# Which engines issue the output stores of the last seven chunks, and which engine evicts the last chunk, in a Fourier-mixing and snake-MLP kernel

## The chip, the cores and the metric

The kernel runs on one core of a Trainium2 chip. The metric is the device time of one execution in microseconds (us). "Faster" and "slower" compare the kernel after the change with the kernel before it. The engines are called here as the profile calls them: PE (TensorE) multiplies matrices, DVE (VectorE) and ACT (ScalarE) work on rows of elements, POOL (GpSimd) does elementwise work and issues DMAs, and SP (SyncE) only issues DMAs and waits. DMAs can be issued by SP, ACT and POOL.

## The reference

The inputs are `x` of 8 x 3008 x 256 and a complex filter for each frequency and channel. Each channel is filtered along the sequence, and the 24,064 tokens that come out go through a two-layer MLP with a snake activation.

```python
X = np.fft.rfft(x, axis=1)
F = (filt_r + 1j * filt_i)[None, :, :]
y = np.fft.irfft(X * F, n=x.shape[1], axis=1)      # 8 x 3008 x 256

h = y.reshape(24064, 256) @ w_in                   # 256 x 2048
s = np.sin(alpha * h)
g = h + s * s / (alpha + 1e-09)
out = (g @ w_out).astype(np.float32)               # 2048 x 256
```

## The kernel before

The transforms are done as matrix products with tables, in two stages of 47 and 64 points, one batch after the other (class `Spectral`). Between the stages the data goes through DRAM scratch buffers, so the spectral part has its own DMAs on SP and POOL. Its result is `y`: channels on partitions, tokens along columns, with room for one pair of batches.

The MLP takes the tokens in 48 chunks, 12 for each pair of batches, each of 512 columns (one of 384 in each pair). For a chunk `k`, `hidden(k, jb)` runs for 16 blocks of 128 hidden units. PE multiplies `w1` by the chunk's columns into the PSUM tile `ph` (L601), ACT takes the cosine as a shifted sine into `cos_all` (L605), and DVE forms `v` from both (L606). The square of the sine is rewritten with the cosine of the doubled angle, and the factors are folded into `w1` and `w2`. `project(k, u)` then multiplies `v` by `w2` into the PSUM tile `po` (L620), 16 matmuls for each tile of 128 tokens. Two token tiles share a `po` tile, which is evicted by one copy into an SBUF tile `o` (L628). Two `po` buffers and three `o` buffers rotate.

The order on every engine is that of the program, written out by hand. A main loop steps through `hidden` of chunk `k` and `project` of chunk `k - 1`, half a block at a time, and between these it puts the steps of the spectral part at due times from a list (`pending`, `slot`). After the last `hidden` there are eight steps with `project` of the last chunk alone. In these, token tiles 2 and 3 are taken in reverse order, and each has a `po` tile, a copy and stores of its own (`final`).

`store` (from L645; its DMAs are issued on L663) writes one tile of 128 tokens to the output. Tokens stand in `y` in the order of the transform, not of the output. A tile is therefore cut into parts whose rows lie at a fixed stride in DRAM, and each part is one DMA with 1 KB per row. There are 2 to 4 parts in a tile, and which engine issues them is the argument `queues`. From the second pair of batches on, a part of `r` row pairs has 2r rows; all stores that the change touches are of this kind. Before, all stores are issued by POOL, except those of the last chunk: its tiles 0 and 1 use SP and POOL by turns, and its tiles 2 and 3 use SP, ACT and POOL by turns, larger parts first.

The program ends on L785: each engine runs a DRAIN, signals, and waits at a barrier that POOL gathers. SP's signal comes after it has waited, one semaphore after another, for the stores that are still out.

Of the kernel before, what the change touches and what calls it, by code (L numbers as in the profile page):

```python
# [71 lines left out]
def kernel(  # L72
# [10 lines left out]
    nc = tc.nc  # L83
# [55 lines left out]
    for h in range(2):  # L139
        nc.sync.dma_start(out=x32[:, 4 * C * h:4 * C * h + 4 * C],  # L140
                          in_=bass.AP(tensor=x.tensor, offset=x.offset + 4 * h * C, ap=[[32 * C, 96], [1, 4 * C]]))
# [182 lines left out]
    al, rest, rec = [w2_cols[0:16, 256 * i:256 * i + 256].bitcast(FP32) for i in range(3)]  # L324
# [32 lines left out]
    for g in range(2):  # L357
        gs = slice(12 * g, 12 * g + 12)
        for k, filt in enumerate((filt_r, filt_i)):
            for q in range(2):  # L360
                if (g, k, q) == (0, 1, 1):
# [3 lines left out]
                    out=f_t[k][64 * k + 32 * q:64 * k + 32 * q + 32, gs, :],  # L365
                    in_=bass.AP(tensor=filt.tensor, offset=filt.offset + off,
                                ap=[[N1 * C, 32], [step, 12], [1, C]]))
# [20 lines left out]
    def one_between():  # L388

        if between:  # L390
            between.pop(0)()
# [143 lines left out]
    for jb in range(0, 16, 8):  # L535
        ins = nc.sync.dma_start(out=w_out32[:, jb:jb + 8],
                                in_=moe_w_out[128 * jb:128 * jb + 1024].rearrange("(b p) c -> p b c", p=128))
# [41 lines left out]
    for step in ([(weights_in, g) for g in range(3)] + [(s1.load_x, 0), (weights_in, 3), (s1.load_x, 1),  # L579
# [8 lines left out]
    chunks = [(pb, c0, 384 if c0 == 2560 else 512) for pb in range(B // 2)  # L588
              for c0 in [*range(0, 2561, 512), *range(2944, 2 * S, 512)]]

    v = {}
    pso = {}
# [17 lines left out]
    def project(k, u):  # L610

        pb, c0, n = chunks[k]
        t, half = divmod(u, 2)
        final = k == len(chunks) - 1 and t > 1
        if final:
            t = 5 - t
        if (t % 2 == 0 or final) and half == 0:
            pso[k] = ops.tile([128, 2, C], FP32, name=f"po_{k}_{t}", tag="o")
        for jb in range(8 * half, 8 * half + 8):
            nc.tensor.matmul(out=pso[k][:, t % 2, :], lhsT=v[k][:, jb, 128 * t:128 * t + 128],  # L620
                             rhs=w2[:, jb, :], start=(jb == 0), stop=(jb == 15))
            if jb % 2:
                one_between()
        last = 128 * (t + 1) == n
        if half == 1 and (t % 2 == 1 or last or final):
            i0 = t % 2 if final else 0
            o = opool.tile([128, 2, C], FP32, name=f"o_{k}_{t}", tag="o")
            nc.scalar.copy(out=o[:, i0:t % 2 + 1, :], in_=pso[k][:, i0:t % 2 + 1, :])  # L628
            for i in range(i0, t % 2 + 1):
                store(o[:, i, :], pb, c0 + 128 * (t - t % 2 + i),  # L630
                      (nc.sync, nc.scalar, nc.gpsimd) if final else (nc.sync, nc.gpsimd) if k == len(chunks) - 1 else
                      (nc.gpsimd,))

    def load_half_table():

# [4 lines left out]
    def runs(cnt):  # L640

        whole = cnt if max(d for d in range(1, 17) if cnt % d == 0) > 7 else cnt - cnt % 16
        return [(0, whole), (whole, cnt - whole)] if 0 < whole < cnt else [(0, cnt)]

    def store(o_blk, pb, col, queues):  # L645

        p, parts = 0, []
        while p < 128:
            odd, rest = divmod(col + p, S)
            n2, row = divmod(rest, NR)  # L650
            cnt = min(128 - p, NR - row)
            t0 = (2 * pb + odd) * S + 32 * row
            if 2 * pb + odd < TILED:
                parts += [(i, rows, t0 + n2 + 32 * r0, p + r0, [[32 * C, rows]])
                          for i, (r0, rows) in enumerate(runs(cnt))]
            else:
                parts += [(i, 2 * rows, t0 + 31 - n2 + 64 * r0, p + 2 * r0, [[64 * C, rows], [(2 * n2 + 1) * C, 2]])
                          for i, (r0, rows) in enumerate(runs(cnt // 2))]
            p += cnt
        if len(queues) == 3:  # L660
            parts = [(i, *part[1:]) for i, part in enumerate(sorted(parts, key=lambda part: -part[1]))]
        for i, rows, t0, p0, ap in parts:
            queues[i % len(queues)].dma_start(  # L663
                out=bass.AP(tensor=out.tensor, offset=out.offset + t0 * C, ap=[*ap, [1, C]]),
                in_=o_blk[p0:p0 + rows, :])
# [81 lines left out]
    for k in range(len(chunks) + 1):  # L747
        for j in range(8):
            if k < len(chunks) and step > 0:
                hidden(k, 2 * j)  # L750
                hidden(k, 2 * j + 1)
            slot(step)
            if k > 0:
                n_half = 2 * (chunks[k - 1][2] // 128)
                for u in range(n_half * j // 8, n_half * (j + 1) // 8):
                    project(k - 1, u)
            slot(step + 0.5)
            step += 1
# [31 lines left out]
```

## Time and profile before

| What | Value |
|---|---|
| runs before | 782.67 us median of 3 (781.52, 782.67, 783.74) |
| profiled execution, first to last instruction (span) | 779.9 us |
| the median of the runs above that span | 2.8 us |
| PE busy | 762.2 us (98% of the span) |
| DVE / ACT / POOL busy | 656.8 / 612.0 / 416.1 us |
| output stores issued by POOL (L663) | 608, mean 561 ns |
| evictions of `po` by ACT (L628) | 97, mean 590 ns |

A span runs from the first to the last instruction on the core. No time of its own is listed for the profiled execution beside this span, so sums are made against 779.9 us and then carried over to the median of the runs, which lies 2.8 us above it. In the tables of the profile, "busy" leaves out instructions of the sequencers: a `q` after an engine's name (SPq, ACTq, POOLq) marks these, among them DMA issues of SP and ACT, waits on semaphores and DRAIN.

### The profile page before, as it was taken

What the parts mean: (1) busy time and instruction counts of PE and PEld (TensorE: products, weight loads), DVE (VectorE), ACT (ScalarE), POOL (GpSimd) and SP (SyncE); (2) the same over time, 40 slices, a digit from 0 to 9 for tenths busy, and PEclk for the clock granted to TensorE, in tenths of its full rate; (3) what the DMA queues carried; (4) which work ended last, traced back from release to release, by engine and by line L of the source; (5) the groups of instructions that cost most, each with busy time, mean ns of one, the idle gap of its engine ahead of it and who ended that gap; (6) DMA issues with size and microseconds to landing.
All of it is one profiled execution on the core that took longest, in us unless ns stands there. A gap on an engine that the chain in (4) does not pass through costs nothing.

```text
span 779.9 us, 17214 instructions
## 1 busy us (share of the span) xinstructions
PE 762.2 (98%) x6039; PEld 517.1 (66%) x6039; DVE 656.8 (84%) x1170; ACT 612.0 (78%) x1206; POOL 416.1 (53%) x727
## 2 busy tenths in 40 slices
PE   8999999999999999999999999999999999999994
PEld 4757766666666667666666666666666666766663
DVE  7887998899988889988889888898888888777771
ACT  6798887898787878878788878888788777777771
POOL 6455455644636456554656555653555545544553
PEclk9999999999999999999999999999999999999998
DMA  9945678854865448553575437654364232411111
GB/s 227 283 103 164 141 164 247 216 131 112 218 147 125 111 94 206 136 135 93 128 191 125 127 98 180 179 133 108 82 156 106 68 86 70 120 36 35 41 41 42
DMA packets 80201, 101.49 MB, mean 130 GB/s; under 512 B 19552, under 2 KB 58494, under 8 KB 80114
## 3 DMA queue, kind: packets, MB, share of 16 engines
q0 software_dynamic: 30096, 50.41, 27.3%
q1 hardware_dynamic: 49719, 49.86, 24.1%
q8 instruction: 47, 0.77, 0.4%
q14 instruction: 40, 0.33, 0.1%
q10 hardware_dynamic: 299, 0.13, 0.1%
HBM read 56.15 MB, written 46.66 MB: 132 GB/s over the span
## 4 chain that ended last, share of the span: by engine, by line
PE 89%; DVE 4%; DMA 2%; ACT 1%; POOL 1%; issue 1%; POOLq 0%; SPq 0%
PE po L620 39%; PE ph L601 39%; DVE v L606 3%; PE pd L316 2%; PE pb L243 2%; PE pa L222 2%; PE pc L293 1%; DMA x<-in_x_dram 1%; DMA d<-t_h 1%; POOL out_dram L663 1%; PE pc L513 1%; ACT cos_all L605 1%; PE warm L437 1%; PE pb L491 1%; DMA cos_all<-in_x_dram 0%
## 5 line engine op out<-in xcount | busy, mean ns | idle before, releaser
L606 DVE SCALAR_TENSOR_TENSOR v<-cos_all,ph 128x512 f16<-128x512 f32 (+1 forms) x768 | 482.8, 672 | 95.9 <-ACT cos_all L605 92.2
L605 ACT ACTIVATE cos_all<-ph 128x512 f32<-128x512 f32 (+1 forms) x768 | 413.7, 599 | 100.2 <-PE ph L601 99.8
L663 POOL DMA_DIRECT2D out_dram<-o x608 | 337.2, 561 | 287.1 <-ACT o L628 256.1
L601 PE MATMUL ph<-y,w 128*128 128x512 f16 (+1 forms) x1536 | 389.0, 375 | 1.3 <-DVE v L606 1.1
L620 PE MATMUL po<-w,v 128*128 128x256 f16 x3008 | 389.3, 273 | 0.0
L620 PEld LDWEIGHTS <-v 128*128 128x128 f16 x3008 | 290.1, 98 | 84.2 <-issue 1.1
L601 PEld LDWEIGHTS <-w 128*128 128x128 f16 x1536 | 143.2, 98 | 113.9 <-issue 19.0
L628 ACT COPY o<-po 128x512 f32<-128x512 f32 (+1 forms) x97 | 57.3, 590 | 13.1 <-PE po L620 9.5
L246 ACT CAST xf<-pb 128x512 f16<-128x512 f32 x84 | 50.9, 606 | 1.3 <-PE pb L243 1.0
L185 ACT CAST y<-pd 128x376 f16<-128x376 f32 (+1 forms) x86 | 41.9, 489 | 12.2 <-PE pd L316 8.8
L160 POOL DMA_DIRECT2D x<-in_x_dram x48 | 25.7, 540 | 38.0 <-DVE v L606 26.6
L185 ACT CAST t_h<-pa 128x512 f16<-128x512 f32 (+1 forms) x60 | 32.9, 589 | 12.7 <-PE pa L222 11.5
L316 PEld LDWEIGHTS <-t_a 96*128 96x128 f16 x448 | 31.4, 97 | 12.7
L264 DVE TENSOR_TENSOR p<-p,xs 128x512 f16<-128x512 f16 x84 | 35.7, 425 | 2.9
L263 DVE TENSOR_TENSOR xs<-xs,filt_t 128x512 f16<-128x512 f16 x84 | 35.2, 419 | 2.1 <-DMA xs<-xf 1.8
L257 DVE TENSOR_TENSOR p<-xf,filt_t 128x512 f16<-128x512 f16 x84 | 35.1, 418 | 0.0
L185 ACT CAST gt<-pc 128x512 f16<-128x512 f32 x54 | 28.1, 594 | 8.4 <-PE pc L293 8.4
L187 DVE CAST t_h<-pa 128x512 f16<-128x512 f32 (+1 forms) x52 | 33.5, 683 | 0.2
L243 PE MATMUL pb<-t,d_t 128*128 128x256 f16 x168 | 32.1, 273 | 0.0
L316 PE MATMUL pd<-wh_t,t_a 96*128 96x94 f16 x384 | 31.8, 204 | 0.0
L235 POOL DMA_DIRECT2D t<-d x28 | 24.5, 877 | 11.9 <-DMA d<-t_h 10.9
L243 PEld LDWEIGHTS <-d_t 128*128 128x128 f16 x168 | 16.3, 98 | 14.3
(69 smaller groups left out, 274.7 us busy)
## 6 DMA issues: line engine op xcount, KB each, us to landing
t<-d POOLq DMA_DIRECT2D x28, 384.0 KB, 5.2
xs<-xf SPq DMA_DIRECT2D x168, 64.0 KB, 2.7
t_a<-d SPq DMA_DIRECT2D x28, 384.0 KB, 5.3
x<-in_x_dram POOLq DMA_DIRECT2D x50, 188.0 KB, 4.7
d<-t_h SPq DMA_DIRECT2D x48, 192.0 KB, 5.1
d<-gt SPq DMA_DIRECT2D x36, 256.0 KB, 3.6
out_dram<-o POOLq DMA_DIRECT2D x106, 64.0 KB, 2.1
out_dram<-o POOLq DMA_DIRECT2D x32, 80.0 KB, 3.5
```

Source lines behind the costliest of these rows:

```text
L185: marks["act"] = nc.scalar.copy(out=dst, in_=src)
L243: nc.tensor.matmul(out=ps[:, i, :], lhsT=d_t[:, s, :], rhs=self.t2[s // 6][:, s % 6, :], start=True, stop=True)
L246: nc.scalar.copy(out=self.xf[u], in_=ps)
L263: nc.vector.tensor_tensor(out=xs, in0=xs, in1=f_t[1][:, 2 * u:2 * u + 2, :], op=ALU.mult)
L264: nc.vector.tensor_tensor(out=p, in0=p, in1=xs, op=ALU.add)
L316: nc.tensor.matmul(out=psv[:, i, :], rhs=wi_t if self.b < TILED else wh_t, start=True, stop=True, lhsT=t4_h[ch // 2][0:NK, n0 % 16 + i, cb ...
L601: nc.tensor.matmul(out=ps[:, 0:n], lhsT=w1[:, cb, jb * 128:jb * 128 + 128], rhs=y_cols[:, cb, c0:c0 + n], start=(cb == 0), stop=(cb == 1))
L605: nc.scalar.activation(out=cs[:, 0:n], in_=ps[:, 0:n], func=AFT.Sin, bias=float(np.pi / 2))
L606: marks["snake"] = nc.vector.scalar_tensor_tensor(out=v[k][:, jb, 0:n], in0=cs[:, 0:n], scalar=-1.0, in1=ps[:, 0:n], op0=ALU.add, op1=ALU. ...
L620: nc.tensor.matmul(out=pso[k][:, t % 2, :], lhsT=v[k][:, jb, 128 * t:128 * t + 128], rhs=w2[:, jb, :], start=(jb == 0), stop=(jb == 15))
L628: nc.scalar.copy(out=o[:, i0:t % 2 + 1, :], in_=pso[k][:, i0:t % 2 + 1, :])
L663: queues[i % len(queues)].dma_start(out=bass.AP(tensor=out.tensor, offset=out.offset + t0 * C, ap=[*ap, [1, C]]), in_=o_blk[p0:p0 + rows, :])
```

## The change

The stores of chunks 41 to 47 (the last seven, `rest < 7`) are no longer issued by POOL. SP issues them alone, except for the last six token tiles: those of tiles 2 and 3 of chunk 46 and of all four tiles of chunk 47 are dealt to SP and ACT by turns, larger parts first. The three copies that evict the last chunk move from ACT to DVE. In the built program 78 stores leave POOL; SP issues 70 more than before (78 instead of 8) and ACT 8 more (10 instead of 2). The last instruction of POOL's own work is then the last store of chunk 40. On SP the new stores stand behind all transfers of the spectral part, and on ACT behind its last cosine. The three copies stand on DVE behind its last `v`. The order on PE is unchanged.

```diff
@@ project
-            nc.scalar.copy(out=o[:, i0:t % 2 + 1, :], in_=pso[k][:, i0:t % 2 + 1, :])
+            rest = len(chunks) - 1 - k
+            copy = nc.vector.tensor_copy if rest == 0 else nc.scalar.copy
+            copy(out=o[:, i0:t % 2 + 1, :], in_=pso[k][:, i0:t % 2 + 1, :])
             for i in range(i0, t % 2 + 1):
                 store(o[:, i, :], pb, c0 + 128 * (t - t % 2 + i),
-                      (nc.sync, nc.scalar, nc.gpsimd) if final else (nc.sync, nc.gpsimd) if k == len(chunks) - 1 else
-                      (nc.gpsimd,))
+                      (nc.sync, nc.scalar) if rest == 0 or (rest == 1 and t > 1) else
+                      (nc.sync,) if rest < 7 else (nc.gpsimd,))
@@ store
-        if len(queues) == 3:
+        if len(queues) > 1:
             parts = [(i, *part[1:]) for i, part in enumerate(sorted(parts, key=lambda part: -part[1]))]
         for i, rows, t0, p0, ap in parts:
             queues[i % len(queues)].dma_start(
```

## The prediction

> **What bounds the kernel now.** I read the page first: which engine is full, and whether it stays full to the end.
>
> ```profile
> PE 762.2 (98%) x6039; PEld 517.1 (66%) x6039; DVE 656.8 (84%) x1170; ACT 612.0 (78%) x1206; POOL 416.1 (53%) x727
> PEclk9999999999999999999999999999999999999998
> ```
>
> PE is the bound and its clock is full. The busy times by stretch split the part that the change touches (columns: length, then busy us and instruction count of PE, PEld, DVE, ACT and POOL, the clock, the DMA share, GB/s):
>
> ```profile
> 689.00:762.00 73.00, 73.00 (x533) 49.84 (x532) 54.09 (x86) 52.02 (x100) 37.52 (x66) 1.00 0.14 39
> 762.00:780.00 18.00, 7.67 (x71) 6.63 (x68) 1.29 (x2) 2.42 (x6) 6.77 (x12) 0.80 0.16 44
> ```
>
> From 689 to 762 us PE is busy for all of 73.00 us. POOL's 66 stores there take 37.52 us beside it, and DVE and ACT have about 20 us of slack each. So nothing that POOL, DVE or ACT save in that stretch shortens it. The last stretch is different: PE works 7.67 of 18 us. What ends when, there, is in the timeline:
>
> ```profile
> 762.30 7.37 PE L620 MATMUL po<-w,v 128*128 128x256 f16 x66
> 763.60 6.19 POOL L663 DMA_DIRECT2D out_dram<-o  x11 [4.03 <-ACT o L628]
> 766.21 0.59 ACT L628 COPY o<-po 128x512 f32<-128x512 f32 x1 [2.91 <-PE po L620]
> 766.82 5.64 SPq L663 DMA_DIRECT2D out_dram<-o  x8
> ...
> 769.70 0.37 ACT L628 COPY o<-po 128x256 f32<-128x256 f32 x1 [1.38 <-DMA out_dram<-o]
> 770.11 1.40 ACTq L663 DMA_DIRECT2D out_dram<-o  x1
> 770.37 0.57 POOL L663 DMA_DIRECT2D out_dram<-o  x1 [0.58 <-ACT o L628]
> ```
>
> PE ends at 769.67, the last copy at 770.07, and the last store is issued by SP until 772.46. The span ends at 779.9. Nothing in this view fills the rest, so I asked for the instructions of the program's end (L785) from 762 to 779 us:
>
> ```profile
> L785 SPq EVENT_SEMAPHORE  x9: 28/28/28, 772.5 to 774.4; - x9
> L785 SPq DRAIN  x2: 7/7/7, 774.4 to 774.5; - x2
> L785 DVEq DRAIN  x1: 836/836/836, 762.5 to 762.5; - x1
> L785 PEldq DRAIN  x1: 2155/2155/2155, 767.6 to 767.6; - x1
> L785 POOLq DRAIN  x1: 8765/8765/8765, 770.3 to 770.3; - x1
> L785 ACTq DRAIN  x1: 213/213/213, 771.5 to 771.5; - x1
> ```
>
> The three numbers are min/median/max in ns, then first and last start. SP has seen every store land and has drained at 774.5. POOL's DRAIN starts at 770.34, takes 8.77 us and ends at 779.11. The barrier follows, 0.8 us to 779.9. So the end is set by POOL: its drain closes 4.6 us after SP, the next latest.
>
> **Part 1: POOL is out of the tail.** After the change POOL's last store is that of chunk 40, in the burst that starts at 676.44 and lasts 7.90 us, so to 684.34. If its DRAIN again takes 8.77 us, it ends at 693.1, some 86 us before the end, and POOL then waits at the barrier. The price of POOL at the end falls from 4.6 us to nothing. If the drain grew tenfold, to 88 us, it would end at 772, still before SP. The 78 stores that it no longer issues (mean 561 ns) are worth nothing more, since PE is full beside them. Next late is SP: with its finish unchanged the span would be 774.5 + 0.8 = 775.3 us, a gain of 4.6.
>
> One rule speaks against this. The Trainium skill, "VectorE: DVE Perf Modes", section "The DRAIN you can't avoid", says that the drains of preamble and postamble take about 12 ns each on all five engines. SP's 7 ns fit that; POOL's 8,765 ns do not, so for POOL the row decides. By the rule there would be no drain to move, and the sum would be SP's own shift below.
>
> **Part 2: SP up to 763 us.** SP gets 66 stores in the eleven half chunks that start from 689.13 to 756.65. Its last transfers of the spectral part are issued at 661.81 for 1.72 us, so nothing stands behind these stores but other stores. The eight SP stores of before take 5.64 us, 0.705 each with their gaps. 66 x 0.705 = 47 us fit in 74.5 us (689.13 to 763.60). Cost nil, hidden under PE; a store that is late only delays the `o` buffer used three half chunks, about 20 us, later. The cover is gone at 74.5 / 66 = 1.13 us a store.
>
> **Part 3: the last six tiles.** For chunk 46, tiles 2 and 3, SP has four stores and ACT three, from 763.3; at 0.705 SP is done by 766.2. For chunk 47 SP has 4 + 2 + 2 = 8, as before, and ACT 4 + 2 + 1 = 7 instead of 2. ACT's stores stand behind its last cosine, and no copy waits behind them any more.
>
> DVE copies: rows of DVE casts from PSUM are 683 ns for 512 columns, 543 for 376 and 344 for 188, so 256 columns come to an estimated 0.42 us by interpolation. ACT took 0.59 and 0.37. The first copy ends 0.1 us later, at 766.89, the last 0.05 later, at 770.12. Behind the copies nothing is queued on DVE, whose last `v` ends at 763.33. PE needs the `po` of tiles 0 and 1 back for its last 16 matmuls, which begin at about 767.9 (16 x 0.109 before 769.67). 1.0 us of cover remains; without it each us late is a us of PE.
>
> SP's tail: 8 x 0.705 from 766.92 gives 772.56, 0.1 later than before. The forms change, though. Before they were 16, 32, 4, 32, 13, 32, 1 and 32 row pairs, now 32, 11, 32, 13, 32, 15, 32 and 2. The store of 13 took 0.913 us, the others 0.567 to 0.692. Pricing 11 and 15 like 13, in place of 16 (0.62) and 4 (0.69), adds 0.5. The last store is smaller, 4 KB, which on POOL landed in 1.7 us; SP's 64 KB take 2.1: up to 0.4 back, of which I take 0.3. So SP ends at 774.5 + 0.1 + 0.5 - 0.3 = 774.8.
>
> The Trainium skill, "DMA: Bandwidth & Descriptors", section "Why a DMA increments its semaphore by 16 and not by 1", says that the issuing sequencer writes the missing increments itself when a store runs on fewer than 16 engines. By it the last store of 2 would be dear too, about 0.3 more; the stores of 1 and 4 at 0.59 and 0.69 speak for little of that.
>
> ACT's tail: seven stores, with 0.687 (16 pairs) and 1.398 (30 pairs) as the only rows. Five at 0.687 and two (15, 30) at 1.398 make 6.2, from 766.92 to 773.1; the last starts at 771.7 and lands in 2.3, at 774.0. It is level with SP's last landing, so SP's end stands.
>
> **Sum.** 774.8 + 0.8 = 775.6 us against 779.9: a gain of 4.3. On the median that is 782.67 - 4.3 = 778.4.
>
> **Bounds.** At SP's fastest row, 0.567, the stores of the last tile wait for the copy at 770.16; the last starts at 770.73, lands in 1.7, and 0.5 of SP's waits and 0.8 follow: 773.7, a gain of 6.2 (776.5). At 0.913 for each of SP's eight the last starts at 773.3, lands in 2.1, and the end is at 776.7: a gain of 3.2 (779.5). At ACT's 1.398 for each of SP's last twelve, from 763.4, the last starts at 778.8 and the end is at 782.2: slower by 2.3 (785.0). The middle is nearest to SP's own eight rows, so I take those. About 0.3%, 2.4 us, is what a measurement of this kernel can tell from no change (its three runs span 2.2 us).
>
> **Rivals.**
> 1. *The drain stays at the end.* POOL's DRAIN may not belong to its own stores but run until about 5.1 us after the last store of any queue has landed (issued at 771.90, landed 2.1 later at 774.0, and 779.1 is 5.1 after that). The time would be as before, 782.7, give or take 0.5. For it: the trace shows no long drain other than this, and none of POOL long after its last store. Against it: SP's drain with the same stores landed takes 7 ns, and this one begins as soon as POOL's stores are issued. Chance 0.05. By the 12 ns of the Trainium skill's page on VectorE, above, the time would come out here too: SP's shift of 0.3 alone (783.0).
> 2. *SP and ACT hinder each other.* Stores on ACT at 770.11 took 1.40 us and on SP at 769.54 0.91, while they overlapped. If fifteen stores in parallel make each of SP's cost 1.1, the four of chunk 46 end at 767.8, the last starts at 775.5, and the end is 778.9: a gain of 1.0 (781.7). Against it: SP's three stores after that took 0.57 to 0.59 beside the same ACT store. Chance 0.05.
> 3. *SP cannot keep the pace* (slower). Above 1.13 us a store the 66 stores outlast their 74.5 us and the backlog lands on the end. At 1.2 they end at 768.3; of the twelve others the last starts at 781.5, and with 2.1, 0.5 and 0.8 the end is at 784.9: 5.0 slower (787.7). For it: SP's `xs<-xf` DMAs, earlier in the kernel, reach 2.15 us (median 0.588). Against it: at a DMA share of 0.14 to 0.16 the row is 0.57 to 0.91. Chance 0.04.
>
> The forecast has 0.86. Faster: the forecast and 0.01 of rival 2, whose milder forms gain over 2.4 us, 0.87. The same: rival 1 and the other 0.04 of rival 2, 0.09. Slower: rival 3, 0.04. The range runs from the fastest row (776.5) to 780.4, past the bound of 0.913 by 0.9 for the spread of the runs; rivals 1 to 3 lie outside.
>
> **What would show it.** Right: POOL's long DRAIN starts near 684 and ends before 700; SP's last DRAIN stands near 774.8 and the span at 775.6; PE full to about 769.7; SP's stores near 0.7 us. Wrong: a POOL DRAIN that still closes near 779 (rival 1), SP's stores at 1.1 us or more in the tail (2) or from 689 on (3), or gaps on PE before 769 behind the copies on DVE.

## The result and the profile after

The kernel after takes 778.35 us (median of 4 runs, 777.96 to 779.97) against 782.49 us before: a ratio of 0.9949, with a 95% interval of 0.9934 to 0.9964, or 4.1 us less. The profiled run has a span of 778.2 us; it is the slowest of the four (779.97 us), and the spans of the other three are 776.2 to 776.8 us.

The busy times by stretch, cut where PE has 7.7 us of work left, have the columns of the table shown for the kernel before:

```profile
689.00:764.70 75.70, 75.70 (x552) 51.54 (x550) 56.54 (x89) 54.72 (x106) 0.00 (x0) 1.00 0.14 38
764.70:778.20 13.50, 7.70 (x71) 6.66 (x68) 2.83 (x5) 1.12 (x3) 0.00 (x0) 0.94 0.22 59
```

POOL is empty from 689 us on, and PE is still full up to its end. The instructions of the program's end (now L787) from 686 to 778 us:

```profile
L787 SPq EVENT_SEMAPHORE  x10: 17/28/28, 776.1 to 777.6; - x10
L787 POOLq DRAIN  x3: 46/98/3118, 686.1 to 777.9; - x3
L787 SPq DRAIN  x3: 7/7/7, 777.3 to 777.7; - x3
```

The long DRAIN, with which POOL closes its own work, starts at 686.1, not near the end, and it is 3.12 us long instead of 8.77. SP is the last to be done, at 777.4, and 0.8 us of barrier follow. The timeline of the tail:

```profile
760.00 16.02 SPq L665 DMA_DIRECT2D out_dram<-o  x16
...
764.38 8.02 PE L620 MATMUL po<-w,v 128*128 128x256 f16 x72
765.45 0.59 ACT L630 COPY o<-po 128x512 f32<-128x512 f32 x1 [0.22 <-PE po L620]
766.07 9.07 ACTq L665 DMA_DIRECT2D out_dram<-o  x10
768.95 0.69 DVE L630 COPY o<-po 128x512 f32<-128x512 f32 x1 [2.88 <-PE po L620]
770.69 0.42 DVE L630 COPY o<-po 128x256 f32<-128x256 f32 x1 [1.05 <-DMA out_dram<-o]
772.50 0.42 DVE L630 COPY o<-po 128x256 f32<-128x256 f32 x1 [1.38 <-DMA out_dram<-o]
```

PE ends at 772.40, 2.7 us later than in the profile before, and yet the span is shorter. The stretch from PE's end to the end of the span is 5.8 us; before it was 10.2 us (769.67 to 779.9). So the tail gave 4.4 us. The later end of PE comes from the opening, which the change does not touch. Busy times by stretch, first before, then after:

```profile
0.00:60.00 60.00, 53.96 (x437) 34.92 (x438) 49.60 (x71) 46.71 (x88) 32.98 (x50) 1.00 0.85 205
60.00:110.00 50.00, 49.55 (x379) 36.38 (x378) 45.37 (x90) 43.08 (x84) 26.83 (x50) 1.00 0.65 155
```

```profile
0.00:60.00 60.00, 53.53 (x423) 33.87 (x424) 48.97 (x71) 44.26 (x83) 30.59 (x46) 0.97 0.83 198
60.00:110.00 50.00, 48.59 (x369) 35.47 (x367) 42.81 (x86) 42.55 (x84) 25.74 (x48) 1.00 0.62 152
```

By 110 us PE has done 24 matmuls fewer in the profile after (792 against 816). Most of the delay is there within the first 15 us: the matmuls of L353 begin at 14.6 us instead of 12.1. The granted clock of the first 60 us was also lower, 0.97 against 1.00, but that is not needed for it: in a second profile of the kernel after it was 1.00, and PE still ended at 772.16. The end of PE differs from run to run: in the fourteen profiles of this study PE ends between 769.57 and 774.32 us. The comparisons below therefore use the stretch from PE's end to the end of the span, called the tail, beside the times.

### The profile page after: what moved, and what is told of

Its sections match the earlier page's. It is cut to its first block, busy times and chain, and to the rows that moved or that the text cites. A ratio compares the mean times of both kernels' runs of the same rounds, so it can differ in the third digit from the quotient of the medians.

```text
span 778.2 us, 17224 instructions
## 1 busy us (share of the span) xinstructions
PE 763.9 (98%) x6039; PEld 517.3 (66%) x6039; DVE 658.2 (85%) x1173; ACT 610.5 (78%) x1203; POOL 371.2 (48%) x649
## 4 chain that ended last, share of the span: by engine, by line
PE 91%; DVE 4%; DMA 2%; ACT 1%; issue 1%; ACTq 0%; POOLq 0%; DVEq 0%
PE po L620 40%; PE ph L601 40%; DVE v L606 3%; PE pd L316 2%; PE pb L243 2%; PE pa L222 2%; PE pc L293 1%; PE pc L513 1%; DMA w<-in_moe_alpha_dram 1%; PE warm L437 1%; DMA d<-t_h 1%; ACT cos_all L605 1%; PE pb L491 1%; DMA t<-d 1%; PE pa L459 1%
## 5 line engine op out<-in xcount | busy, mean ns | idle before, releaser
L665 POOL DMA_DIRECT2D out_dram<-o x530 | 292.5, 558 | 241.8 <-ACT o L630 212.6
L630 ACT COPY o<-po 128x512 f32<-128x512 f32 x94 | 55.9, 595 | 7.6 <-PE po L620 7.3
L185 ACT CAST t_h<-pa 128x512 f16<-128x512 f32 (+1 forms) x60 | 32.8, 589 | 12.5 <-PE pa L222 11.3
```

The source lines that it names most:

```text
L185: marks["act"] = nc.scalar.copy(out=dst, in_=src)
L665: queues[i % len(queues)].dma_start(out=bass.AP(tensor=out.tensor, offset=out.offset + t0 * C, ap=[*ap, [1, C]]), in_=o_blk[p0:p0 + rows, :])
```

## Experiments

All are short edits of the kernel before or after. "POOL DMAs" counts all DMAs that POOL issued in the run; "last POOL DMA issued" is the end of the issue; "drain" is the time from the end of the issue of its last DMA to the end of its long DRAIN.

| Kernel | POOL DMAs | last POOL DMA issued | drain, us | DRAIN ends | PE ends | span ends | tail, us |
|---|---|---|---|---|---|---|---|
| before | 704 | 770.95 | 8.16 | 779.11 | 769.67 | 779.90 | 10.23 |
| after | 626 | 687.07 | 2.13 | 689.20 | 772.40 | 778.19 | 5.79 |
| after, again | 626 | 686.81 | 2.13 | 688.94 | 772.16 | 778.16 | 6.01 |
| DVE evicts only | 704 | 772.57 | 8.16 | 780.73 | 771.18 | 781.52 | 10.34 |
| stores only | 626 | 687.62 | 2.14 | 689.75 | 772.96 | 779.93 | 6.97 |
| one store on POOL | 627 | 771.44 | 2.25 | 773.69 | 770.05 | 775.47 | 5.42 |
| last chunk only | 699 | 767.44 | 7.75 | 775.20 | 769.57 | 775.98 | 6.41 |
| tail on POOL, fewer earlier | 638 | 771.21 | 2.77 | 773.99 | 769.94 | 775.50 | 5.56 |
| eleven chunks on SP | 573 | 627.44 | 7.35 | 634.78 | 771.32 | 777.23 | 5.91 |
| 78 small DMAs added | 704 | 722.95 | 8.16 | 731.11 | 771.02 | 776.83 | 5.81 |
| SP alone | 626 | 686.26 | 2.14 | 688.40 | 771.60 | 784.55 | 12.95 |
| before plus 28 DMAs | 732 | 772.82 | 10.45 | 783.27 | 771.55 | 784.06 | 12.51 |
| POOL shares last chunk | 630 | 775.71 | 2.39 | 778.10 | 774.32 | 779.04 | 4.72 |
| two more chunks on SP | 604 | 771.95 | 9.88 | 781.83 | 770.57 | 782.61 | 12.05 |

### The two halves of the change

The kernel before, with DVE as the engine of the last evictions:

```diff
-            nc.scalar.copy(out=o[:, i0:t % 2 + 1, :], in_=pso[k][:, i0:t % 2 + 1, :])
+            copy = nc.vector.tensor_copy if k == len(chunks) - 1 else nc.scalar.copy
+            copy(out=o[:, i0:t % 2 + 1, :], in_=pso[k][:, i0:t % 2 + 1, :])
```

> The kernel before with one part of the change: DVE evicts the last chunk; POOL keeps its stores. Theory (POOL's DRAIN sets the end): POOL's last store still comes near PE's end + 0.7 us and the DRAIN still closes some 9.4 us after PE's end, so the stretch from PE's end to the end of the span stays at 10.2 us, give or take 0.2, and the time is that of before (782.5, within 0.3%). Rival (the eviction by DVE carries the gain): the stretch falls to about 6 us and the time to about 778.5.

Measured: 782.07 us against 781.96, ratio 1.000 (0.9974 to 1.0027). The instructions of the program's end:

```profile
L786 POOLq DRAIN  x3: 46/98/8762, 772.0 to 781.2; - x3
```

The long DRAIN is where it was, 8.76 us, and the eviction by itself brings nothing.

The kernel after, with ACT evicting throughout:

```diff
-            copy = nc.vector.tensor_copy if rest == 0 else nc.scalar.copy
+            copy = nc.scalar.copy
```

> The kernel after with ACT evicting the last chunk as before; the stores move as in the change. Theory (POOL's DRAIN): nearly the whole gain. From PE's end to the end of the span 5.8 to 6.5 us (5.78 after, 10.23 before), since the last two copies can queue behind ACT's stores of 0.7 us each; time 778.4 to 779.0. Rival (the eviction by DVE carries the gain): 10.2 us and 782.5.

Measured: 778.82 us, ratio 0.9951 (0.9928 to 0.9974). POOL's DRAIN is out of the tail, which is 6.97 us. The stores carry the gain. The tail is 1.0 to 1.2 us longer than in the two profiles of the kernel after, more than expected. The timeline shows a reason:

```profile
770.58 3.08 ACTq L665 DMA_DIRECT2D out_dram<-o  x4
773.76 0.37 ACT L630 COPY o<-po 128x256 f32<-128x256 f32 x1 [3.21 <-DMA out_dram<-o]
```

Four stores stand ahead of this copy on ACT. On DVE in the kernel after the same copy began at 770.69, 1.7 us before PE's end; here it begins at 773.76, 0.8 us after PE's end at 772.96. In this profile, then, eviction by DVE would be worth about 1 us, and only once ACT issues stores. The times do not show it: 0.9951 here and 0.9949 for the kernel after, with intervals wide enough to hide 1 us.

### What the length of POOL's DRAIN goes by

The kernel after, with one store of two row pairs in the last tile back on POOL:

```diff
+                      (nc.sync, nc.scalar, nc.gpsimd) if final and t == 2 else
                       (nc.sync, nc.scalar) if rest == 0 or (rest == 1 and t > 1) else
```

> The kernel after, but the smallest part (2 row pairs) of the very last tile is issued by POOL, as it was before. It asks what the length of POOL's DRAIN goes by: it took 8.77 us before (8.2 after the last POOL store was issued) and 3.12 us after the change (2.1 after the last POOL store). Theory 1 (a late DRAIN on POOL is long whatever came before it): the one store brings it back; POOL's DRAIN ends 8.2 us after that store, the stretch from PE's end to the end is 10.2 us, time 782.5. Theory 2 (the length goes by the POOL stores of the last few us): the DRAIN ends about 2 us after the store, before SP is done, the stretch is 5.5 to 5.8 us and the time 778.4.

Measured: 777.57 us, ratio 0.9934 (0.9913 to 0.9955).

```profile
L788 POOLq DRAIN  x3: 46/98/2853, 770.8 to 775.2; - x3
```

The DRAIN begins in the tail again, but it is 2.85 us long and ends before SP does. A late store on POOL is not enough for a long DRAIN.

Only the last chunk's stores off POOL:

```diff
-                      (nc.sync, nc.scalar) if rest == 0 or (rest == 1 and t > 1) else
-                      (nc.sync,) if rest < 7 else (nc.gpsimd,))
+                      (nc.sync, nc.scalar) if rest == 0 else (nc.gpsimd,))
```

> The kernel after with the stores of chunks 41 to 46 back on POOL; only chunk 47 goes to SP and ACT. POOL's last store (chunk 46) is then issued about 2.1 us before PE ends. Theory 1 (a late DRAIN ends 8.2 us after POOL's last store): it ends 6.1 us after PE's end, 1.1 later than SP does in the kernel after, and the stretch from PE's end to the end is about 6.9 us, time 779.5. Theory 2 (2.1 us after the last store): it ends with PE, SP sets the end, 5.6 to 5.8 us, time 778.3. If the six chunks on SP cost or gained something by themselves under PE, the time would differ from this by that amount.

Measured: 778.63 us, ratio 0.9945 (0.9921 to 0.9969).

```profile
L786 POOLq DRAIN  x3: 46/98/8837, 766.4 to 775.7; - x3
```

It is long here: it ends 7.75 us after the last store (the theories had 8.2 and 2.1), though no POOL store comes after 767.44. It sets the end: 775.20 against SP's 774.5. At that point the two runs left a choice: the stores of the last few us (7 here, 1 in the run before, but 14 close together ahead of 3.12 us in the kernel after, which spoke against it), or the number of POOL's DMAs in the whole run. The next three separate them.

The last six tiles exactly as before, POOL included; the 66 stores from chunk 41 to the first half of chunk 46 on SP:

```diff
                       (nc.sync, nc.scalar, nc.gpsimd) if final else (nc.sync, nc.gpsimd) if k == len(chunks) - 1 else
+                      (nc.sync,) if len(chunks) - 8 < k < len(chunks) - 2 or (k == len(chunks) - 2 and t < 2) else
                       (nc.gpsimd,))
```

> The kernel before, its last six token tiles on SP, ACT and POOL exactly as before and evicted by ACT, so POOL's last store comes as late as ever; only the 66 stores of chunk 41 to the first half of chunk 46, which lie under PE, go to SP. So far POOL's DRAIN ended, after its last store was issued, 8.16 us with 704 DMAs on POOL in the whole run (before), 7.75 with 699, 2.25 with 627, 2.13 with 626 (after). Theory (its length goes by the number of POOL's DMAs so far, 0.077 us for each, starting near 598): 638 DMAs, 3.1 us after the last store, so it ends before SP does; from PE's end to the end 5.6 to 6.2 us, time 778.0 to 778.6, nearly the whole gain. Rival (a DRAIN is long when POOL was issuing stores up to the end): 8.2 us, 10.2 us from PE's end, 782.

Measured: 777.68 us, ratio 0.9931 (0.9910 to 0.9952).

```profile
L786 POOLq DRAIN  x3: 46/98/3372, 770.6 to 775.2; - x3
```

POOL's twelve stores of the tail come as late as in the kernel before, and still the DRAIN is 3.37 us. The whole gain is there with POOL's tail untouched.

Now the number alone, on the kernel after:

```diff
+    dummy = pool("dummy", 1, DRAM).tile([16, 78, 4], FP32, name="dummy")
+    def dummy_store(i):
+        nc.gpsimd.dma_start(out=dummy[:, i, :], in_=id32[:, 0:4])
+    for i in range(78):
+        put(337 + 0.1 * i, dummy_store, i)
```

> The kernel after, and on POOL 78 added DMAs of 16 x 16 bytes from SBUF to a DRAM scratch, right behind its last store of chunk 40: POOL's DMAs are 704 again, as before, but its last one comes about 40 us before PE's end. Theory (count of DMAs, whatever they carry): the DRAIN ends 8.2 us after the last of them, near 740 us. By bytes or descriptors moved instead: 2.1 to 3.5 us. The time is that of the kernel after, since all of it lies under PE.

```profile
L796 POOLq DRAIN  x3: 46/98/10421, 720.7 to 776.6; - x3
```

Measured: 778.64 us in one run. From the last DMA's issue to the DRAIN's end it is 8.16 us, the figure of the kernel before to 0.01, for 704 DMAs of which 78 carry 256 bytes each. It ends at 731.11, 40 us before PE does. So from 626 to 704 DMAs the DRAIN goes by the number of DMAs that POOL has issued, not by what they carry, how late they are, or whether the other engines still work.

Fewer DMAs than in the kernel after:

```diff
-                      (nc.sync,) if rest < 7 else (nc.gpsimd,))
+                      (nc.sync,) if rest < 11 else (nc.gpsimd,))
```

> The kernel after with four more chunks (37 to 40) stored by SP, so that POOL issues about 573 DMAs in all, 53 fewer than after. It asks what lies under the start near 598. Count from a floor: the DRAIN ends within 0.6 us of POOL's last store. Count that starts anew every so many DMAs: it is long again, 6 us or more. Either is hidden here; the end goes by SP and the stretch from PE's end is 5.6 to 6 us. If stores of chunk 37 and 38 hold up the spectral transfers on SP, PE shows gaps from 620 to 665 us and the whole is some us slower.

```profile
L787 POOLq DRAIN  x3: 46/98/8408, 626.4 to 777.0; - x3
```

Measured: 779.0 us in one run. With 573 DMAs the DRAIN is long again, 7.35 us. The count must start anew somewhere. The groups of instructions from 640 to 680 us show what stores on SP cost while it still has spectral transfers:

```profile
L316 PE MATMUL pd<-wh_t,t_a 96*128 96x94 f16 x24 | 2.0, 205 | 0.8 <-DMA t_a<-d 0.8
```

PE waits 0.8 us for `t_a`. The same group in the same stretch of the kernel after has no such wait:

```profile
L316 PE MATMUL pd<-wh_t,t_a 96*128 96x94 f16 x24 | 2.0, 204 | 0.0
```

I took the new start to come about every 120 DMAs, and put that to the test on the kernel before, with 28 of the small DMAs added to POOL in the same way:

> The kernel before, unchanged but for 28 added DMAs of 16 x 16 bytes on POOL from SBUF to a DRAM scratch, behind the stores of chunk 40 and so under PE: POOL issues 732 DMAs instead of 704. So far the DRAIN ended, after POOL's last store, 7.35 us with 573 DMAs, 2.13 with 626, 2.77 with 638, 7.75 with 699 and 8.16 with 704: a rise of about 0.077 a DMA with one fall between 573 and 626, as of a count that starts anew about every 120 DMAs (478, 598, 718). Theory: at 732 the count has started anew, the DRAIN is about 1 to 1.5 us, SP sets the end, 5.5 to 5.8 us from PE's end, and the time falls to about 778.3 though POOL does more. Rival (the length rises with the number of DMAs without end, and 573 had another reason): 8.16 + 28 x 0.077 = 10.3 us, 12.4 from PE's end, 784.5.

```profile
L794 POOLq DRAIN  x3: 46/98/11048, 772.2 to 783.8; - x3
```

Measured: 785.31 us, ratio 1.0029 (1.0013 to 1.0044). My theory fell: there is no new start at 718, and the rival's 10.3 us and 12.4 us of tail came out at 10.45 and 12.5. Twenty-eight DMAs of 256 bytes, hidden under PE, lengthen the kernel by 2 us.

The last run went back below 626, with the three-queue form of the next section and two more chunks on SP:

```diff
-                      (nc.sync,) if rest < 7 else (nc.gpsimd,))
+                      (nc.sync,) if rest < 9 else (nc.gpsimd,))
```

> The last chunk dealt to SP, ACT and POOL as in the run with three queues, and two more chunks (39 and 40) stored by SP: POOL issues 604 DMAs instead of 630, its last one as late as ever. A line through the nine profiles from 626 to 732 DMAs is 0.0785 us a DMA and reaches zero at 600. Theory (the count starts anew at some DMA shortly before the 600th, and from there a DMA costs 0.078): at 604 the DRAIN ends 0.3 to 0.5 us after the last store; from PE's end to the end 4.6 to 4.9 us, as with 630, since SP sets the end; time 777.5 to 778.5. Rival (the start lies nearer to 626, and 604 still counts from the one before, by 573 at 7.35): 9.8 us, 11.3 from PE's end, about 784.

```profile
L788 POOLq DRAIN  x3: 46/98/10475, 771.4 to 782.3; - x3
```

Measured: 784.39 us, ratio 1.0026 (0.9989 to 1.0063), so the time cannot be told from that of the kernel before; the gain is gone. Again the rival held: the DRAIN ended 9.88 us after the last store (9.8 expected), with a tail of 12.05 (11.3 expected). If the count is all that matters, 573 and 604 lie on one line (0.082 us a DMA, drawn through these two points alone) and 626 to 732 on another (0.078 us a DMA). The new start then lies between the 604th and the 626th DMA of this program, and just after it some of the count is already there: the second line would reach zero at 600. What sets the place of the new start stays open. The run with 732 DMAs shows none at 718, but it does not exclude a distance near 120: the two lines reach zero at about 483 and 600, 117 apart, and by that distance the start after the one between 604 and 626 would lie between 721 and 743, perhaps beyond 732. Descriptors or bytes were not tried for it.

### The tail without ACT, and with POOL

SP alone:

```diff
-                      (nc.sync, nc.scalar) if rest == 0 or (rest == 1 and t > 1) else
                       (nc.sync,) if rest < 7 else (nc.gpsimd,))
```

> The kernel after without ACT's share: SP alone issues the stores of the last six tiles, 22 of them from about 6.4 us before PE ends. At the 0.76 us that SP's 78 stores took on average in the kernel after, they last 16.7 us, the last starts 9.6 us after PE's end and lands 1.9 us later; with SP's waits and the barrier (1.0) the stretch from PE's end to the end is about 12.4 us, 6.6 more than after: 785, slower than before by 0.3%. Rival (SP and ACT share one rate, so that the split gains nothing): 6 to 7 us and 779.

Measured: 786.2 us, ratio 1.0032 (1.0014 to 1.0049). The timeline from 767 us:

```profile
766.67 15.54 SPq L664 DMA_DIRECT2D out_dram<-o  x20
```

Twenty stores in 15.54 us, 0.78 each, and a tail of 12.95 us. ACT's share is worth 7 us of tail: more than the 4.6 us that POOL's DRAIN cost at the end of the kernel before. SP and ACT do not share one rate.

Three queues for the last chunk:

```diff
+                      (nc.sync, nc.scalar, nc.gpsimd) if rest == 0 else
-                      (nc.sync, nc.scalar) if rest == 0 or (rest == 1 and t > 1) else
+                      (nc.sync, nc.scalar) if rest == 1 and t > 1 else
                       (nc.sync,) if rest < 7 else (nc.gpsimd,))
```

> The kernel after, but the stores of the last chunk are dealt to SP, ACT and POOL by turns: 7, 4 and 4 of them instead of SP 8 and ACT 7. POOL issues 630 DMAs. Theory (count): its DRAIN ends about 2.4 us after its last store, earlier than SP is done; SP's last store starts about 1 us earlier than in the kernel after, so from PE's end to the end 4.8 to 5.3 us (5.8 after) and 777.5. Rival (any store of POOL in the tail costs its long DRAIN): 10 us, 782.5.

Measured: 778.2 us, ratio 0.9934 (0.9911 to 0.9958). The kernel after, on the same chip:

> The kernel after itself, on the same chip as the two others, for comparison: 778.4, 5.8 us from PE's end to the end, the DRAIN 3.1 us near 686.

Measured: 778.69 us, ratio 0.9944 (0.9923 to 0.9965). The three-queue form has the shortest tail of all, 4.72 us against 5.8 and 6.0, and SP's last store is issued 1.3 us after PE's end (775.64 and 774.32), against 2.9 us in the kernel after (775.33 and 772.40). The two times cannot be told apart by their intervals; the profiled run of the three-queue form also had the latest end of PE (774.32).

## Why the prediction was right, step by step

**POOL out of the tail: right, with one term wrong.** The forecast was a gain of 4.3 us with SP as the next bound. The tail gave 4.4, and the times 4.1. The two halves of the change, run alone, confirm where it came from. The marks set for the profile (SP's last DRAIN at 774.8, the span 775.6, PE full to 769.7) came 2.6 to 2.7 us later, all by PE's later end; counted from PE's end they hold within 0.2 us. The step "if its DRAIN again takes 8.77 us" failed: it took 3.12, and the runs show that this length goes by the number of POOL's DMAs. It did no harm, since the DRAIN ended 88 us before SP was done (689.20 and 777.42). But the prediction gave the gain to the place of POOL's last store alone. The run with POOL's tail untouched shows that fewer DMAs on POOL do as much, and the run with 28 more shows that the same tail can also get worse.

**The rivals.** Rival 1 (the DRAIN stays about 5.1 us behind the last landing) is refuted by the kernel after, where it ends at 689.20. So is, for POOL, the 12 ns of the Trainium skill's "VectorE: DVE Perf Modes", section "The DRAIN you can't avoid": POOL's DRAIN at the end of its work took 2.85 to 11.05 us in these profiles, though for SP the 7 ns are near it. Rival 2 (SP and ACT hinder each other) would have ended 9.2 us after PE; it was 5.8, and SP alone was worse. Rival 3 (SP cannot keep the pace) needed 1.13 us a store; the mean was 0.763, and 0.81 from start to start where one store followed directly on another.

**SP's price.** The stores of the output on SP and ACT from 691 us on:

```profile
L665 SPq DMA_DIRECT2D out_dram<-o x78: 407/778/1688, 691.6 to 775.3; - x78
L665 ACTq DMA_DIRECT2D out_dram<-o x10: 635/750/1472, 766.1 to 774.3; - x10
```

SP's median is 0.78 us, the mean 0.763. The prediction took 0.705 from eight stores, most of which had 16 or 32 row pairs. Its figure includes the gaps between the stores; without them it is 0.647. Like for like that term was 18% too low, with no effect under PE.

**SP's tail.** Eight stores were to take 6.14 us (5.64 and 0.5 for the forms); they took 6.36, from 769.67 to 776.02. SP was to be done 5.1 us after PE (774.8 and 769.67) and was done 5.0 after (777.42 and 772.40). The parts were sized less well than the sum. The forms of 11 and 2 row pairs, one after the other in the view of the stores by narrow windows:

```profile
L665 SPq DMA_DIRECT2D out_dram<-o x1: 817/817/817, 770.3 to 770.3; - x1
...
L665 SPq DMA_DIRECT2D out_dram<-o x1: 689/689/689, 775.3 to 775.3; - x1
```

Eleven took 0.82, 13 and 15 took 0.84, near the 0.91 that the prediction used; 2 took 0.69, in the place of the store of 1 that the sum had at 0.59. On SP the forms of 16 and 32 pairs were the cheap ones of this tail (0.59 to 0.61) and all others dearer. This would fit the rule of the Trainium skill, "DMA: Bandwidth & Descriptors", section "Why a DMA increments its semaphore by 16 and not by 1", that the issuing sequencer writes the missing increments itself, though the 2 pairs were dearer by 0.1 and not by 0.3, and the shortest of SP's 78 stores, 0.41 us at 747.75, had 1 pair.

The 0.3 that was to come back for a small last store did come back, and more: from the start of the last store to SP's DRAIN it was 2.09 us (775.33 to 777.42), against 2.59 before (771.90 to 774.49). Only 0.1 of it is the landing (1.9 against 2.0); the rest is SP's waits behind the landing, 0.2 us against 0.6. Against that stand the gaps between the eight stores, 0.78 us against 0.46, which the sum had left as they were; 0.37 of them lies right before the last store. So it is in part luck that the sum came within 0.1 us.

**DVE's copies.** They took 0.69 and 0.42, as interpolated. The prediction booked them as 0.1 lost. By the one profile with stores only they are worth 1.0 to 1.2 us of tail, which the times do not confirm; that ACT's copies would have stood behind its stores was seen and not priced.

## What to carry to other kernels

Read the tail by the instructions of the program's end, not by the last store: an engine that looks idle can hold the end with its DRAIN. In this kernel the DMAs issued by GpSimd left such a DRAIN, whose length went up with their number and fell once in between. So its last DMA should come well before the others are done, or the count be watched when the tail is measured. When stores pile up at the end, deal them to two or three queues, and do not let an eviction stand behind them on the engine that issues them.

## What the runs showed of the hardware that was not expected

- In this program POOL's DRAIN at the end of its work took 0.078 us for each of its DMAs beyond about the 600th (626 to 732 DMAs: 2.13 to 10.45 us after the last one), and 0.082 on another line below (573: 7.35, 604: 9.88). Small DMAs counted like large ones: 8.16 us at 704 in each of three profiles, in one of them with 78 DMAs of 256 bytes, and in the middle of the run.
- On SP, a store of 32 row pairs took about 0.6 us, and one of 15 about 0.86. On POOL the two took 0.55 and 0.56.
- ACT's first store of a form other than 16 or 32 row pairs took 1.40 us before (30 pairs) and 1.47 after (15 pairs); its later ones took 0.64 to 0.87. Over the thirteen profiles in which ACT issues such stores the first took 1.30 to 1.65 us. The price of 1.398 in the prediction was that of a first one.
